# A gated mix of two attentions: one matmul per 128-row tile and PSUM bank for numerators and weight folds, where there were two

## The chip, the core and the metric

The kernel runs on one core of a Trainium2 chip. The core has five engines that run side by side, each through its own list of instructions in order: TensorE (PE) multiplies matrices, VectorE (DVE), ScalarE (ACT) and GpSimd (POOL) work on elements, SyncE (SP) issues DMAs. PE writes to PSUM, eight banks of 512 float32 columns; DVE and ACT read PSUM, POOL does not. The metric is the device time of one execution in microseconds (us); the lower the better.

## What is computed

Both halves take the same input x of 2048 tokens by 640 features, 32 heads of 20 features each.

```python
qkv = x @ wqkv                                   # half A: q, k, v by heads
pq, pk = q @ w_phi, k @ w_phi                    # per head, 20 x 20
phi = concat(softmax(p), softmax(-p))            # of pq and of pk
kv, z = phi_k^T v, sum over tokens of phi_k      # per head
a = ((phi_q @ kv) / (phi_q . z + 1e-6)) @ wo
...
# half B: four segments of 512 tokens; causal softmax attention within a segment,
# mixed per head (sigmoid(beta)) with a linear attention over the segments before; times its own wo
out = g * a + (1 - g) * b                        # g = sigmoid(sum(x * gate_w)) per token
```

All inputs and the output are bfloat16.

## The kernel before, in words

The kernel is one long program with no loops left at run time. The order of the instructions on each engine is the order in which the code emits them (a manual schedule over all engines); strings in the code spell out that order by hand.

**The 640 features as tiles and banks.** 640 features are five tiles of 128 rows (`KC = 5`, index `j`). Heads are 20 features wide, so a tile does not begin or end with a head: tile 0 holds heads 0 to 6, tile 1 heads 6 to 12, tile 2 heads 12 to 19, tile 3 heads 19 to 25, tile 4 heads 25 to 31 (`TH`, L62). Head 6 lies partly in tile 0 and partly in tile 1; heads 12, 19 and 25 are split in the same way. A product over all heads with a block-diagonal right side therefore takes, per tile, only the columns of that tile's heads, and the split heads need a sum over two tiles. The result of 640 columns lies in two PSUM banks, 16 heads (320 columns) each; tile 2 spans both.

`PIECES` (L63) lists these products: tile, bank, first head, end head. A product with `start` clears its bank's marks and writes; one without it follows in the same bank. In the list of before, a head that the tile before has begun is a product of its own (20 columns, added to what is there), and the heads that are new are another product. That makes ten products: 140, 20, 120, 20, 60 columns in bank 0 and 80, 20, 120, 20, 120 in bank 1. `FIRST` and `LAST` (L65) name the products that open and close a bank.

**Where the list is used.** `emit_foldM` (L186) multiplies a tile of a transposed weight matrix with the block-diagonal `w_phi` (`Wphi`), so that the projections deliver `pk` and `pq` at once; it is called ten times. Five calls are at the start for the keys (L317 on, steps M0, M2, M1, M4, M3; ACT casts each result into `WkA` at L194), five for the queries after the last key step (L348 on; ACT casts into `WqA`). `emit_num` (L477) multiplies a tile of the exponentials of the queries (`Eqs`) with the block-diagonal `kv` (`kvn`) for a chunk of 128 tokens and one sign: 16 chunks by 2 signs, 32 calls.

**What stands around the folds.** At the start PE transposes five tiles of the key weights (L182), with the folds in between, then multiplies x by the folded key weights and by the value weights, 16 steps of 20 products (L240). ACT takes the exponentials (L251) and copies the values (L253), DVE sums and takes reciprocals (L255, L258), POOL normalises (L259). After the sixteenth step come the five query folds, then the products `kv` (`emit_kv`, L394: short products of two column groups), in among them and after them the query products (`emit_pq`, L421) with their exponentials on ACT (L428). SP moves the normalised keys into `Z` (L267), DVE adds them (L275), and PE transposes the sum (L280).

**What stands around the numerators** (L647 to L706). In each of the 32 steps (chunk, sign) DVE scales a numerator (`emit_tt`, L531, into a tile `tt` with two buffers), PE does half of a projection for half B (five products of 320 columns, L561, which ACT casts at L621) and the numerator three steps ahead (three PSUM tiles of two banks: `nps0`, `nps1`, `nps2`). After both signs POOL adds the two halves (`oA`, L691) and SP transposes the sum. The denominators of the next batch of four chunks are made by PE behind two of the numerators (`emit_den`, L500), DVE takes their reciprocal (L507, L508) and that of their sum (L512, L694), and POOL makes the scale of the next batch from them (L522, L524), which `emit_tt` of the next batch needs. Then half B follows: scores on PE (L770), exponentials on ACT (L774), masks on POOL (L781), products with the values (L824), and the projections and outputs in between (L948, L1008).

Of the kernel before, what the change touches and what calls it, by code (L numbers as in the profile page):

```python
# [15 lines left out]
def kernel(  # L16
# [43 lines left out]


    TH = [(P * j // DH, (P * j + P - 1) // DH + 1) for j in range(KC)]  # L62
    PIECES = [(0, 0, 0, 7), (1, 0, 6, 7), (1, 0, 7, 13), (2, 0, 12, 13), (2, 0, 13, 16),  # L63
              (2, 1, 16, 20), (3, 1, 19, 20), (3, 1, 20, 26), (4, 1, 25, 26), (4, 1, 26, 32)]
    FIRST, LAST = {0, 5}, {4, 9}  # L65
    HW = 8

    gS = res.tile([P, NCH], F32, name="gS")
# [31 lines left out]
    for what in "c w1 w3 x0 x1 g v0 v1".split():  # L100
        n = int(what[1:]) if len(what) > 1 else 0
# [74 lines left out]
    def w2tile(name):  # L176
        return aps.tile([P, 2, 512], F32, name=name, tag="w2")
# [8 lines left out]
    def emit_foldM(WT, dst, ic, eng=nc.scalar.copy):  # L186
        ps = w2tile("fold_ps")
        for n, (j, bk, lo, hi) in enumerate(PIECES):
            h0 = TH[j][0]
            nc.tensor.matmul(ps[:, bk, (lo - 16 * bk) * DH:(hi - 16 * bk) * DH],  # L190
                             lhsT=WT[:, j, ic * P:(ic + 1) * P],
                             rhs=Wphi[:, j, lo - h0:hi - h0, :].rearrange("p h d -> p (h d)"),
                             start=(n in FIRST), stop=(n in LAST))
        eng(out=dst[:, ic, :].rearrange("p (b n) -> p b n", b=2), in_=ps[:, :, 0:320])  # L194

    def emit_xT(n):
# [120 lines left out]
    for step in "P T0a T2d M0a T1d M2a T4d T3d M1a X0 M4a X1 M3a k0 g k1 v0 v1 r0 r1".split():  # L317
        n = int(step[1:2] or 0)
        if step[0] == "T":
            emit_foldT(wnat_k, WkT, n, {"a": nc.scalar.copy, "d": nc.vector.tensor_copy}[step[2]])  # L320
        elif step[0] == "M":
            emit_foldM(WkT, WkA, n, {"a": nc.scalar.copy, "d": nc.vector.tensor_copy}[step[2]])
        elif step[0] == "X":
            emit_xT(n)
        elif step[0] == "P":
            for j in (0, 2):
                emit_Wphi(j, nc.vector)
        elif step[0] == "k":
            emit_a1_mm(n, pks, WkA, 320)
        elif step[0] == "v":  # L330
            emit_a1_mm(n, pvs, WvA, 321)
        elif step[0] == "r":
            emit_a1(n)
            emit_zmove(n)
        else:
            emit_gw()
# [11 lines left out]
    for n in range(KC):  # L348
        emit_foldM(WkT, WqA, n)
# [127 lines left out]
    def emit_num(ch, sgn):  # L477
        qb, qc = divmod(ch, HB // P)
        t = nps[(2 * ch + sgn) % 3].tile([P, 2, 512], F32, name="num")
        for n, (j, bk, lo, hi) in enumerate(PIECES):  # L480
            h0 = TH[j][0]
            nc.tensor.matmul(t[:, bk, (lo - 16 * bk) * DH:(hi - 16 * bk) * DH],  # L482
                             lhsT=Eqs[qb, j][:, sgn, qc * P:(qc + 1) * P],
                             rhs=kvn[:, sgn, j, lo - h0:hi - h0, :].rearrange("p h e -> p (h e)"),
                             start=(n in FIRST), stop=(n in LAST))
        return t

    def num_view(t):
# [161 lines left out]
    def emit_num_at(i):  # L650
        if i < len(order):
            ch, sgn = order[i]
            t = nums[ch, sgn] = emit_num(ch, sgn)
            if ch % 4 == 1 and ch < NCH - 4:
                for n in range(2):
                    emit_den(den_view(t)[:, n], ch + 3 + 2 * sgn + n)
# [55 lines left out]
    with ExitStack() as bctx:  # L712
# [487 lines left out]
        for ps, lo in quarters:  # L1200
            for k5 in range(KC):
                nc.tensor.matmul(ps, lhsT=oT4[:, 2, k5, :], rhs=WoB[:, k5, lo:lo + 160],
                                 start=(k5 == 0), stop=(k5 == KC - 1))
# [36 lines left out]
```

## Time and profile before

| what | value |
|---|---|
| three runs | 314.25, 313.38, 314.42 us |
| their median | 314.25 us |
| the profiled execution's own time | 314.52 us |
| its span | 312.8 us, 9844 instructions |
| granted TensorE clock | 1.0 |
| products at L482 (numerators) | 320, first and last start at 88.8 and 126.0 us |
| products at L190 (folds) | 100, first and last start at 5.2 and 55.1 us |

How to read the lines that follow. The page's first part gives for each engine the busy time, its share of the span and the number of instructions; PE is the matmuls, PEld the weight loads that belong to them. A group of instructions is shown with line, engine, operation, the tile that is written and the tiles that are read, shapes, count, busy time in us and mean duration of one in ns, then the idle time of the engine just before. The timeline gives start and duration in us, engine, line, operation, tiles, shapes and count, and in brackets the idle time before and what ended it. The chain of waits goes back from the last instruction to what released each one; its rows are start, duration, engine, tile, line and count. Where a distance between the starts of two single matmuls is given, it is from the start times in the same trace.

### The profile page before, as it was taken

The page shows a single profiled execution, that of the slowest core. Times are in us where ns is not written, and L with a number is a line of the kernel's source. Part 1 is how long each engine was busy: PE and PEld are TensorE (multiplying, and loading weights), DVE is VectorE, ACT ScalarE, POOL GpSimd, SP SyncE. Part 2 cuts the span into 40 slices and gives each one's busy share as a digit, 9 for nine tenths or more (in the row PEclk, how much of TensorE's full clock was granted, in tenths as well). Part 3 has the DMA queues.
Part 4 walks back from the last instruction along what each step waited for, and adds up shares of the span by engine and source line. Part 5 has one row for each costly group of instructions (what it writes and reads, how often), then busy time and mean ns, then how long its engine had stood idle before and what let it go on. Part 6 is the DMA issues. An engine that isn't in the chain of part 4 may idle for free.

```text
span 312.8 us, 9844 instructions
## 1 busy us (share of the span) xinstructions
PE 302.4 (97%) x4038; PEld 205.3 (66%) x4038; DVE 230.3 (74%) x532; ACT 251.9 (81%) x320; POOL 205.6 (66%) x310
## 2 busy tenths in 40 slices
PE   8999999999999999999999999999999999999995
PEld 7788877855578788465656666666666666544573
DVE  3477997998779997767758588788656746667773
ACT  4677888357956549899999899999998999899953
POOL 8588599103346989965666667688886767756560
PEclk9999999999999999999999999999999999999999
DMA  7989934439217998775331358343855556334142
GB/s 223 202 173 188 234 103 127 130 88 365 76 27 99 129 142 132 153 103 105 37 69 36 69 111 121 57 91 61 110 92 90 53 106 116 82 82 97 40 115 84
DMA packets 97414, 35.33 MB, mean 113 GB/s; under 512 B 85722, under 2 KB 97370, under 8 KB 97370
## 3 DMA queue, kind: packets, MB, share of 16 engines
q1 hardware_dynamic: 96794, 34.06, 56.3%
q10 hardware_dynamic: 576, 0.66, 0.7%
q8 instruction: 31, 0.51, 0.7%
q14 instruction: 13, 0.11, 0.1%
HBM read 6.10 MB, written 2.62 MB: 28 GB/s over the span
## 4 chain that ended last, share of the span: by engine, by line
PE 68%; ACT 21%; DVE 5%; POOL 3%; issue 2%; ACTq 0%; DVEq 0%; POOLq 0%
ACT PT L774 18%; PE proj L1008 10%; PE st_ps L770 9%; PE proj L948 8%; PE pq L421 7%; PE pk L240 7%; PE pv L240 7%; PE nda L824 5%; PE proj L561 3%; DVE tt L531 2%; PE num L482 2%; PE kv_ps L394 2%; DVE rr L507 2%; POOL oA L691 1%; PE warm L316 1%
## 5 line engine op out<-in xcount | busy, mean ns | idle before, releaser
L774 ACT ACTIVATE PT<-st_ps 128x1024 bf16<-128x1024 f32 x160 | 153.9, 1024 | 11.3 <-PE st_ps L770 8.9
L781 POOL TENSOR_SCALAR_AFFINE_SELECT PT<-PT 128x512 bf16<-128x512 bf16 (+1 forms) x130 | 83.8, 663 | 42.7 <-ACT PT L774 42.3
L259 POOL TENSOR_TENSOR EkSn<-Ek,krec 128x1280 bf16<-128x1280 bf16 x15 | 35.1, 2358 | 9.2 <-DVE krec L258 7.3
L824 PEld LDWEIGHTS <-PT 128*128 128x128 bf16 x1040 | 32.9, 96 | 7.8 <-issue 4.5
L1008 PEld LDWEIGHTS <-xTf 128*128 128x128 bf16 x300 | 26.5, 97 | 14.1 <-issue 5.5
L824 PE MATMUL nda<-vB,PT 128*128 128x21 bf16 x1000 | 34.2, 173 | 0.0
L1014 DVE CAST Z<-proj 128x320 bf16<-128x320 f32 x44 | 21.2, 489 | 16.4 <-PE proj L1008 15.3
L428 ACT ACTIVATE Eq<-pq 128x1024 bf16<-128x1024 f32 x20 | 19.4, 1021 | 12.6 <-PE pq L421 12.6
L255 DVE TENSOR_REDUCE ksum<-Ek 128x64 f32<-128x1280 bf16 x16 | 23.6, 1475 | 7.2 <-ACT Ek L251 7.2
L948 PE MATMUL proj<-WkA,oTA 128*128 128x320 bf16 x160 | 28.3, 300 | 0.0
L531 DVE TENSOR_TENSOR tt<-num,rr 128x640 f32<-128x640 f32 x32 | 25.0, 813 | 4.4 <-POOL rr L524 1.7
L770 PE MATMUL st_ps<-Z 32*128 32x512 bf16 (+3 forms) x256 | 25.2, 299 | 3.0 <-ACT PT L774 2.5
L691 POOL TENSOR_TENSOR oA<-tt 128x640 bf16<-128x640 f32 x16 | 24.6, 1546 | 5.2 <-DVE tt L531 5.0
L770 PE MATMUL st_ps<-Eq 32*128 32x384 bf16 (+3 forms) x256 | 25.6, 298 | 1.9 <-ACT PT L774 1.5
L251 ACT ACTIVATE Ek<-pk 128x640 bf16<-128x640 f32 x32 | 20.8, 703 | 8.1 <-PE pk L240 7.0
L240 PEld LDWEIGHTS <-xTf 128*128 128x128 bf16 x200 | 22.6, 113 | 4.7
L421 PE MATMUL pq<-xTf,WqA 128*128 128x512 bf16 x100 | 22.4, 379 | 0.3 <-issue 0.3
L948 PE MATMUL proj<-WvA,oT 128*128 128x320 bf16 x120 | 21.2, 300 | 0.0
L948 PEld LDWEIGHTS <-oTA 128*128 128x128 bf16 x160 | 13.5, 97 | 8.6 <-issue 4.6
L561 PEld LDWEIGHTS <-xTf 128*128 128x128 bf16 x180 | 15.8, 97 | 4.6
L770 PEld LDWEIGHTS <-Z 32*128 32x128 bf16 x256 | 7.5, 91 | 16.2 <-issue 15.0
L482 PEld LDWEIGHTS <-Eq 128*128 128x128 bf16 x320 | 15.9, 96 | 3.3 <-issue 0.7
(194 smaller groups left out, 584.8 us busy)
## 6 DMA issues: line engine op xcount, KB each, us to landing
Z<-EkSn SPq DMA_DIRECT2D x32, 160.0 KB, 2.8
out_dram<-orow SPq DMA_DIRECT2D x8, 160.0 KB, 1.8
out_dram<-oTA SPq DMA_DIRECT2D x6, 160.0 KB, 1.8
WvA<-in_A_wqkv_dram SPq DMA_DIRECT2D x2, 400.0 KB, 5.9
WvB<-in_B_wv_dram SPq DMA_DIRECT2D x1, 800.0 KB, 4.6
WkB<-in_B_wk_dram SPq DMA_DIRECT2D x1, 800.0 KB, 6.4
WqB<-in_B_wq_dram SPq DMA_DIRECT2D x1, 800.0 KB, 8.1
WkA<-in_A_wo_dram SPq DMA_DIRECT2D x1, 800.0 KB, 11.2
```

The costliest lines, as they stand in the source:

```text
L240: nc.tensor.matmul(ps[:, bk, 0:n], lhsT=key_tokens(c, sc), rhs=rhs, start=(c == 0), stop=(c == by_row[-1][0] if sc == 0 and W is WkA else ...
L259: (nc.vector if sc == NCH - 1 else nc.gpsimd).tensor_tensor(out=EkSn[:, sc].rearrange("p s (h f) -> p (s h) f", f=DH), in0=Ek.rearrange("p ...
L421: nc.tensor.matmul(pq[:, half, :], lhsT=WqA[:, c, j * P:(j + 1) * P], rhs=xq[:, 2 * qb + half, c], start=(c == 0), stop=(c == KC - 1))
L531: nc.vector.tensor_tensor(out=tt[:, sgn].rearrange("p (b h) d -> p b h d", b=2), in0=ps, in1=csb, op=ALU.mult)
L561: nc.tensor.matmul(ps, lhsT=xq[:, sc // 4, cc, sc % 4 * P:(sc % 4 + 1) * P], rhs=W[:, cc, half * 320:(half + 1) * 320], start=(cc == 0), s ...
L691: nc.gpsimd.tensor_tensor(out=oA.rearrange("p (h d) -> p h d", d=DH), in0=tt[:, 0], in1=tt[:, 1], op=ALU.add)
L770: nc.tensor.matmul(ps[:, i - i0, o:o + L - c * P], lhsT=kT[32 * i:32 * i + 32, c * P:(c + 1) * P], rhs=qT[32 * i:32 * i + 32, c * P:L], st ...
L774: nc.scalar.activation(out=PT[:, i0:i0 + 2], in_=ps, func=ACT.Exp, scale=SCALE_B)
L781: nc.gpsimd.affine_select(out=v, in_=v, pattern=[[0, n_i], [1, P]], compare_op=ALU.is_ge, fill=0.0, base=0, channel_multiplier=-1)
L824: nc.tensor.matmul(nd[:, j, i], lhsT=block(st, c)[:, i, (j - c) * P:(j - c + 1) * P], rhs=vB[:, c, 4 * st.g + i, :], start=(c == 0), stop= ...
L948: nc.tensor.matmul(ps, lhsT=oT[:, k % KC], rhs=W[:, k % KC, hs], start=(k == 0), stop=(k == n - 1))
L1008: nc.tensor.matmul(ps, lhsT=xq[:, sc // 4, k, sc % 4 * P:(sc % 4 + 1) * P], rhs=W[:, k, half * 320:(half + 1) * 320], start=(k == 0), stop ...
```

## The change

The list of products has six entries in place of ten: for each tile and bank, all heads of that tile that lie in the bank. Where the tile before has begun the first head, the product adds in that head's 20 columns and writes in the other columns, in one matmul. `FIRST` and `LAST` follow the new numbering. The matmuls of both functions carry `skip_group_check=True`. The columns in all stay 720 for each call; all other instructions stay, in their order.

```diff
     TH = [(P * j // DH, (P * j + P - 1) // DH + 1) for j in range(KC)]
-    PIECES = [(0, 0, 0, 7), (1, 0, 6, 7), (1, 0, 7, 13), (2, 0, 12, 13), (2, 0, 13, 16),
-              (2, 1, 16, 20), (3, 1, 19, 20), (3, 1, 20, 26), (4, 1, 25, 26), (4, 1, 26, 32)]
-    FIRST, LAST = {0, 5}, {4, 9}
+    PIECES = [(0, 0, 0, 7), (1, 0, 6, 13), (2, 0, 12, 16), (2, 1, 16, 20), (3, 1, 19, 26), (4, 1, 25, 32)]
+    FIRST, LAST = {0, 3}, {2, 5}
...
@@ emit_foldM
                              rhs=Wphi[:, j, lo - h0:hi - h0, :].rearrange("p h d -> p (h d)"),
-                             start=(n in FIRST), stop=(n in LAST))
+                             start=(n in FIRST), stop=(n in LAST),
+                             skip_group_check=True)
...
@@ emit_num
                              rhs=kvn[:, sgn, j, lo - h0:hi - h0, :].rearrange("p h e -> p (h e)"),
-                             start=(n in FIRST), stop=(n in LAST))
+                             start=(n in FIRST), stop=(n in LAST),
+                             skip_group_check=True)
```

## The prediction

> **What bounds the kernel now.** I read the page first, then the timeline of TensorE (PE), VectorE (DVE), GpSimd (POOL) and ScalarE (ACT) in the stretches where the edited lines run, and the chain of waits last.
>
> ```profile
> PE 302.4 (97%) x4038; PEld 205.3 (66%) x4038; DVE 230.3 (74%) x532; ACT 251.9 (81%) x320; POOL 205.6 (66%) x310
> q8 instruction: 31, 0.51, 0.7%
> ```
>
> PE is busy 97% of the span, but ends are modelled, so I go by starts. The second line is code: 31 packets, 0.51 MB. Over PE's 8076 instructions that is 63 bytes each, so queue 8 feeds PE, and one packet (16.4 KB) holds some 256 instructions, or 128 pairs of weight load and matmul. That matters below.
>
> The edited products, from the lines of the whole span, shapes kept apart:
>
> ```profile
> L482 PE MATMUL num<-kvn,Eq 128*128 128x120 bf16 x96 | 14.5, 213 | 0.0
> L482 PE MATMUL num<-kvn,Eq 128*128 128x20 bf16 x128 | 13.3, 173 | 0.0
> L190 PE MATMUL fold_ps<-Wphi,WkT 128*128 128x120 bf16 x30 | 4.7, 223 | 0.0
> L190 PE MATMUL fold_ps<-Wphi,WkT 128*128 128x20 bf16 x40 | 4.5, 183 | 0.0
> ```
>
> The 168 products of 20 columns are the ones to go: 128 at L482, 40 at L190. Their 173 ns is latency, not price; the price is the distance to the next start. In PE's timeline a numerator group of ten starts at 117.06 and the next work at 117.44. The starts inside it are 61, 28, 52, 26, 26, 35, 27, 52, 26 and 51 ns apart for 140, 20, 120, 20, 60, 80, 20, 120, 20 and 120 columns. So 20 columns cost 26 to 28 ns, 120 cost 52, 140 cost 61, and 60 cost as little as 20.
>
> Who sets the pace of the numerator stage (89 to 127 us) shows in DVE's timeline:
>
> ```profile
> 100.56 2.33 DVE L531 TENSOR_TENSOR tt<-num,rr 128x640 f32<-128x640 f32 x3 [0.55 <-POOL rr L524]
> ...
> 110.50 2.33 DVE L531 TENSOR_TENSOR tt<-num,rr 128x640 f32<-128x640 f32 x3 [0.57 <-POOL rr L524]
> ...
> 120.43 3.06 DVE L531 TENSOR_TENSOR tt<-num,rr 128x640 f32<-128x640 f32 x4 [0.56 <-POOL rr L524]
> 124.74 3.05 DVE L531 TENSOR_TENSOR tt<-num,rr 128x640 f32<-128x640 f32 x4 [1.25 <-POOL oA L691]
> ```
>
> A batch of four chunks takes 9.94 and 9.93 us, and in it DVE stands only in the waits for POOL that the brackets show. PE, in its timeline, waits for DVE:
>
> ```profile
> 116.00 0.54 PE L482 MATMUL num<-kvn,Eq 128*128 128x140 bf16 x10 [0.24 <-DVE uu L508]
> ```
>
> By the starts this wait is 0.40 us (the row before is modelled to run on), and 0.25 at 106.05. The loop DVE, POOL, DVE is the bound there; PE is close behind.
>
> **The change, part by part.** (1) *A product of 140 columns that writes and adds.* No row shows a mixed one. From below: 61 ns, the plain 140 row; it cannot be under the 52 ns of 120 columns. From above: 78 ns, the pair it replaces. Products that write and those that add have one price here (five products of 320 columns at L561 are 135, 135, 135, 136, 136 ns apart, the first of them writing), so I take 61. A group then takes 61+61+35+35+61+61 = 314 ns in place of 384: **0.07 us**, for 42 groups 2.9 us of PE. What counts is where it lies.
>
> (2) *The five folds of the key weights (5.2 to 9.4 us).* The chain of waits is PE with one ACT step here. Three groups run at the fast pace (7.63, 8.29, 8.95): 3 x 0.07. The first two (5.24, 6.38) run at half pace, 617 and 647 ns by starts: there 20+120 columns take 127 ns and 140 would take 117, so 4 x 10 ns each; and since the pace changes at a time and not at a product (about 7.2), half of that remains, 0.04 together. Gain 0.25. Cover: the keys' first product needs the last cast of WkA, which ACT ends at 10.23; its ninth matmul starts at 10.43. They move to about 10.12 and 10.18, so no new wait, with 0.06 to spare. After that PE is dense to 55 us, a step of 20 products each 2.73 us; the next input, a DMA transpose for the third step, lands at 14.1 for a need at 15.0. So 0.25 arrives.
>
> (3) *The five query folds (53.2 to 55.3).* 5 x 0.07 = 0.35 on PE, beside ACT. From 52.14 ACT is dense (two exponentials, a copy, five casts of WqA) until 57.12, and PE's fourth key-value tile waits for the last cast. In the chain:
>
> ```profile
> 53.45 0.69 ACT vA L253
> 54.15 1.27 ACT WqA L194 x3
> 55.79 1.34 ACT WqA L194 x2
> 57.18 4.00 PE kv_ps L394 x175
> ```
>
> Gain 0. It would be 0.35 were ACT faster.
>
> (4) *Code.* In the key-value burst that follows, matmuls start 18 ns apart, so a block of 128 lasts 2.3 us. PE stops in the query product right after it, waiting for nothing that the profile knows:
>
> ```profile
> 61.11 1.69 PE L421 MATMUL pq<-xTf,WqA 128*128 128x512 bf16 x7
> 63.05 0.81 PE L421 MATMUL pq<-xTf,WqA 128*128 128x512 bf16 x3 [0.26 <-issue]
> ```
>
> By starts 0.42 us is lost ahead of matmul 733 (counted from the first), and 0.12 ahead of matmul 605: 128 apart, one block. Queue 8's packets ran 55.97 to 57.42 and 60.27 to 61.52; PE went on at 58.8 and 63.05, 1.4 and 1.5 us after each ended. So from entering a block until the next is usable takes about 4.2 us (58.8 to 63.05). PE's sequencer leads by some 17 matmuls: at 50.86 it took the semaphore instruction of the query folds (matmul 426) while PE was at 409. Hence the block at 477 was entered when PE was at 460, at 54.75, and usable 4.0 later.
>
> The change takes 40 pairs out ahead of this burst, so the block limits fall on work that is now 517, 645 and 773. The first is entered with PE at 500, on today's clock 56.07; the next is usable at 60.1; PE is at 645 at 58.70 + 40 x 0.0184 = 59.43. **It stops for 0.65.** The one after is usable at 64.3, and PE gets to 773 at 60.1 + 1.47 + 0.13 + 2.16 + 0.77 = 64.6: no stop. So 0.65 for today's 0.54: a loss of 0.1. Ends: with no lead 0.95, with a refill of 3.7 us 0.35, so -0.2 to +0.4. Elsewhere blocks last 7 us or more.
>
> On the page "Runtime: NRT & Kernel Launch" (Instruction fetch mechanics) the Trainium skill gives PE's store as 2048 instructions, refilled in blocks of 256, and calls the crossing mostly hidden. The block agrees with 63 bytes x 256; the hiding does not agree with the gap of 0.42. By that page the folds' gain would stay whole.
>
> (5) *The 32 numerator groups: 2.2 us of PE.* Groups one and two end ahead of two projection halves, and the third group starts at 91.00 because ACT ends the last query exponential at 90.95: nothing. The third group and its denominators release the next tt at 92.15 (1.13 us idle): 0.07. From there to 124.7 the loop of DVE and POOL sets the pace, and 28 groups' 2.0 us turn into longer waits of PE. The last group starts at 125.62, held by the tt that waited for POOL's oA (the row at 124.74); after it come one projection and the next stage: 0.07.
>
> Sum on the path: -0.25 - 0.07 - 0.07 + 0.1 = **-0.3 us**. From 127 us on nothing is edited and all moves along. Of the profiled execution, 314.52 (span 312.8 and 1.7 around it), that leaves 314.2; the median shown is 314.25, 0.27 lower, and I carry the difference over: **314.0**. The three runs spread over 1.04 us, 0.33%, so about 0.3% (0.94 us) is what a measurement tells from no change.
>
> **Rivals.** *The code gaps vanish* (the limits fall kindly, or the refill is faster): -0.39 - 0.54 = -0.93, 313.3. For: the refill's first part varied (1.1 to 1.5 us). Against: a block in the burst lasts far less than any refill. Chance 0.15.
>
> *Crossings are hidden, and the 0.42 has another cause and stays*: -0.39, 313.9. For: no row names the cause. Against: the distance of exactly 128. This is what the skill's page above would give. Chance 0.12.
>
> *PE sets the numerator stage after all*: then up to 28 x 0.07 = 2.0 more, 312.0. For: in the chain PE holds 116 to 127 us almost alone. Against: DVE's rows above, and PE's waits for it. Chance 0.08.
>
> *Slower by a longer code stop*: should the moved limits meet two late refills, 1 us at 645 and 0.8 at 773, that is 1.8 - 0.54 - 0.39 = +0.9, 315.1. It makes the kernel slower from a sum of stops of 0.93. For: the refill would be asked for while the moves of Z load the DMA engines (56.4 to 60.6). Against: PE's ten long query products give 2.16 us before 773. Chance 0.15.
>
> *A mixed product costs as much as its pair*: only the limits of code move, +0.1 at most; without fewer instructions 314.25. For: no row shows one. Against: the equal prices in (1). Chance 0.05. That a product without the clearing flag adds where a cell was written and overwrites where it was not, I take from "PSUM — Partial Sum Buffer" (Terms) of the Trainium skill; no run here shows it yet.
>
> **Numbers.** My forecast (313.6 to 314.4) has 0.45. The range, 313.0 to 315.0, takes in the vanished gaps, the hidden crossings and the noise of the median, and leaves out the PE-bound case and the worse half of the longer stop. Faster by over 0.3%: the PE-bound case, half of the vanished gaps, some noise: 0.22. Slower: most of the longer stop and noise: 0.15. Within: 0.63.
>
> **What would show it.** Right: 192 products at L482, 60 at L190, PE x3870, no 20 columns; groups of 0.31 us; batches still 9.9 us apart at the same three rows of DVE with PE's waits for DVE longer, near 0.8 at the two places; the keys' products 0.25 earlier; the casts of WqA still dense; a stop of PE near the end of the key-value burst and none in the query product. Wrong: batches shorter than 9.8; a stop there of over 1 us or none; query folds that bring the key-value products forward.

## The result and the profile after

The changed kernel took 313.21 us (median of 22 runs, 312.93 to 314.31), the kernel before 313.96 in the same session (22 runs, 313.28 to 314.68): a ratio of 0.998, 95% interval 0.9973 to 0.9988. It is 0.75 us faster, 0.2%, which is inside the 0.3% that I had called no change. It lies in my range (313.0 to 315.0), under the 313.6 to 314.4 of my forecast, and next to the 313.3 of the rival in which the code gaps vanish. Two more sets of the unedited kernel are among the experiments; over all three the medians are 313.24 (46 runs) against 313.98 (74 runs), 0.74 us.

The profiled execution of the changed kernel took 313.52 with a span of 311.8 (before 314.52 and 312.8). The first part of its page, engines and the code queue:

```profile
PE 299.6 (96%) x3866; PEld 201.9 (65%) x3870; DVE 230.2 (74%) x532; ACT 251.2 (81%) x320; POOL 205.6 (66%) x310
q8 instruction: 30, 0.49, 0.7%
```

The weight loads show 168 products fewer; PE's 3866 are four short of them, records that the trace lacks. One packet of code less came in. The lines of the whole span, shapes apart, for the edited products (folds are now L189, numerators L482):

```profile
L482 PE MATMUL num<-kvn,Eq 128*128 128x140 bf16 x128 | 15.1, 224 | 1.5 <-DVE uu L509 1.1 <-DVE tt L532 0.2
L482 PE MATMUL num<-kvn,Eq 128*128 128x80 bf16 x64 | 7.5, 199 | 0.0
...
L189 PE MATMUL fold_ps<-Wphi,WkT 128*128 128x140 bf16 x40 | 4.4, 228 | 0.4 <-ACT WkT L183 0.2
L189 PE MATMUL fold_ps<-Wphi,WkT 128*128 128x80 bf16 x20 | 2.4, 200 | 0.0
```

No product of 20 columns is left. The first line has 1.5 us of waits, mostly for DVE, where before's row of this width had 0.3. In DVE's timeline the batches stand as they stood:

```profile
99.75 2.33 DVE L532 TENSOR_TENSOR tt<-num,rr 128x640 f32<-128x640 f32 x3 [0.55 <-POOL rr L525]
...
109.67 2.33 DVE L532 TENSOR_TENSOR tt<-num,rr 128x640 f32<-128x640 f32 x3 [0.55 <-POOL rr L525]
...
119.59 3.06 DVE L532 TENSOR_TENSOR tt<-num,rr 128x640 f32<-128x640 f32 x4 [0.55 <-POOL rr L525]
...
123.90 3.07 DVE L532 TENSOR_TENSOR tt<-num,rr 128x640 f32<-128x640 f32 x4 [1.25 <-POOL oA L692]
```

They are 9.92 and 9.92 us apart, and the waits for POOL are the same. PE's saved time became PE's wait, in its own timeline:

```profile
105.24 0.48 PE L482 MATMUL num<-kvn,Eq 128*128 128x140 bf16 x6 [0.55 <-DVE uu L509]
...
115.16 0.47 PE L482 MATMUL num<-kvn,Eq 128*128 128x140 bf16 x6 [0.55 <-DVE uu L509]
```

By the starts these waits are 0.72 us each, 0.25 and 0.40 before. A group's six starts are 61, 60, 35, 35, 63 and 61 ns apart, 0.31 us to the next work: **a product that writes and adds costs what a plain one of 140 columns costs.**

The stop for code is there, at another place. PE's timeline in the key-value burst (L394) and the query product behind it:

```profile
56.32 2.29 PE L394 MATMUL kv_ps<-vA,EkSn 128*128 128x140 bf16 x108
59.17 1.67 PE L394 MATMUL kv_ps<-vA,EkSn 128*64 128x80 bf16 x81 [0.55 <-issue]
60.77 2.33 PE L421 MATMUL pq<-xTf,WqA 128*128 128x512 bf16 x9
```

By starts 0.72 us is lost, ahead of matmul 605 as forecast (0.65), and none in the query product.

**Where the time went.** I cut the span at four events: K, the keys' first product; C, ScalarE's first cast of the query weights; G, the key-value product behind the ten query products; S, the first score product of the next stage. In us:

| profiled execution | K at | K to C | C to G | stops in C to G (at matmuls 605, 733) | G to S |
|---|---|---|---|---|---|
| before | 9.34 | 44.70 | 9.65 | 0.12, 0.42 | 63.08 |
| changed | 8.45 | 44.68 | 9.81 | 0.72, 0 | 62.93 |

So K to C is untouched, the numerators gave 0.15 (forecast 0.07 + 0.07), the code cost 0.16 (forecast 0.1), and the first nine microseconds gave 0.89 where I had 0.25. That was the first riddle. The second: if this execution still stops for 0.72 us, what do the others do that are faster (25 of the 46 took less than 313.42, down to 312.77)?

### The profile page after: what moved, and what is told of

Same layout as the page of the kernel before. It is cut to its first block, busy times and chain, and to the rows that moved or that the text cites. A ratio compares the mean times of both kernels' runs of the same rounds, so it can differ in the third digit from the quotient of the medians.

```text
span 311.8 us, 9504 instructions
## 1 busy us (share of the span) xinstructions
PE 299.6 (96%) x3866; PEld 201.9 (65%) x3870; DVE 230.2 (74%) x532; ACT 251.2 (81%) x320; POOL 205.6 (66%) x310
## 4 chain that ended last, share of the span: by engine, by line
PE 65%; ACT 21%; DVE 6%; POOL 4%; issue 2%; ACTq 0%; DVEq 0%; POOLq 0%
ACT PT L775 18%; PE proj L1009 10%; PE st_ps L771 10%; PE proj L949 8%; PE pk L240 7%; PE pq L421 7%; PE pv L240 7%; PE nda L825 5%; DVE tt L532 3%; POOL oA L692 2%; PE kv_ps L394 2%; DVE rr L508 2%; PE proj L562 1%; PE num L482 1%; PE warm L316 1%
## 5 line engine op out<-in xcount | busy, mean ns | idle before, releaser
L1009 PE MATMUL proj<-WkB,xTf 128*128 128x320 bf16 x110 | 18.0, 300 | 0.0
```

The lines of the kernel that those rows point to most:

```text
L1009: nc.tensor.matmul(ps, lhsT=xq[:, sc // 4, k, sc % 4 * P:(sc % 4 + 1) * P], rhs=W[:, k, half * 320:(half + 1) * 320], start=(k == 0), stop ...
```

## The experiments

Theory A: the products give what they cost (0.2 in the key folds, 0.14 at the numerators' two ends, nothing in the query folds), and what is beyond that is code: 40 pairs fewer ahead of the burst move the block limits off places that cost 0.54 us. Theory B: fewer products give the whole gain, wherever the limits lie. This is the form that both had from e9 on; the expectations of the runs ahead of it say what A and B meant there. The ratios are those on record, from all executions of a set; they are not quotients of the medians.

**One part at a time.** The list of ten and the list of six are both kept, and each use picks one:

```diff
+        pieces, FIRST, LAST = SIX if dst is WkA else TEN    # e1_keys: key folds alone
+        pieces, FIRST, LAST = TEN if dst is WkA else SIX    # e2_queries: query folds alone
...
+        pieces, FIRST, LAST = SIX                           # e3_nums: numerators alone, folds TEN
```

> Only the five key folds use the six products; query folds and numerators keep ten. Theory A (the prediction's: 0.07 us a group, 0.25 us for the keys on the path; the surplus of the whole change, measured 0.75 us against 0.3, is chance in when TensorE goes from half to full pace in the profiled execution): -0.25 for the folds, and 20 pairs of code fewer ahead of the key-value burst, so a stop of about 0.7 us ahead of matmul 605 and none at 733 (+0.15): -0.1 us, ratio 0.9997. Theory B (the key folds themselves make the full pace come sooner, so the surplus belongs to them): -0.5 to -0.6 us, ratio about 0.9983.

Measured 313.27 against 314.01, ratio 0.9977 (0.9967 to 0.9987), and no stop at all in the profile, where I had expected one of 0.7. The edit takes 20 pairs out ahead of the burst, and it alone gives what the whole change gives. That is nearer to the 0.9983 of B as it stood there (the key folds make the full pace come sooner); the clock times further down speak against that B.

> Only the five query folds use the six products. By the prediction their 0.35 us lie beside ScalarE's dense casts: 0, and the code's limits move by 20 pairs as in the run with the keys alone: a stop of about 0.7 us ahead of matmul 605, none at 733: +0.15 us, ratio 1.0005. Rival (TensorE sets the pace there): -0.35 + 0.15 = -0.2 us, and the key-value products start 0.35 us earlier against the last cast of WqA.

Measured 313.59 against 314.01, ratio 1.0002 (0.9984 to 1.002): by itself unresolved, since three of its 12 executions, at 315.2 to 315.7, show a mean granted clock of 0.993, as the profiled execution of e3 does, which had a stretch at half of TensorE's clock (told below); the other nine have a median of 313.58. The profile has no stop, against what I expected, and took 312.96. ScalarE's casts stayed dense, so the query folds themselves gave nothing.

> Only the 32 numerator groups use the six products; all folds keep ten, so nothing before 88 us changes, the stops of 0.12 and 0.42 us at matmuls 605 and 733 included. By the prediction 0.07 us at the third group and 0.07 us at the last: -0.14 us, ratio 0.9995, with batches still 9.9 us apart. Rival (TensorE sets the numerator stage): -2.2 us, ratio 0.993. If the surplus of the whole change sat here: about -0.6 us.

Measured 314.13 against 314.01, ratio 1.0004 (0.9987 to 1.0021). Nothing moves ahead of the burst here, and both stops are there: 0.37 and 0.41 us. G to S is 62.94, as in the changed kernel. The 0.14 is in the profile and too small for the times.

**Idle products that shift the limits.** Short products whose result lies in PSUM columns that nothing reads stand behind the query folds, where PE waits for ScalarE anyway. In e4_fill14, 14 of them behind the third and the fifth fold of the changed kernel:

```diff
+        for _ in range(14 if dst is WqA and ic in (2, 4) else 0):
+            nc.tensor.matmul(ps[:, 0, 340:356], lhsT=WT[:, 0, ic * P:(ic + 1) * P],
+                             rhs=Wphi[:, 0, 0:1, 0:16].rearrange("p h d -> p (h d)"),
+                             start=True, stop=True, skip_group_check=True)
         eng(out=dst[:, ic, :].rearrange("p (b n) -> p b n", b=2), in_=ps[:, :, 0:320])
```

> The changed kernel with 14 idle products of 16 columns (into unused columns of the fold's own PSUM tile) after the third and after the fifth query fold, where TensorE waits for ScalarE. 28 pairs of code come back ahead of the key-value burst, so the block limits at matmuls 605 and 733 fall on work 28 pairs earlier than in the changed kernel. If the stop is code (theory A): the stop at 605 shrinks from 0.72 to about 0.25 us, none at 733, and the time is 0.4 to 0.5 us below the changed kernel, about 312.8 us. If the stop has another cause at a fixed piece of work: it stays 0.7 us at the same product, and the time is that of the changed kernel or up to 0.1 us more.

Measured 313.23 against 314.01, ratio 0.9979 (0.9965 to 0.9994), no stop. Already 12 pairs off the limits of before there is none; my model of the refill had 0.25. The time is that of the changed kernel, and not the 312.8 expected, which took the stop of 0.72 for the rule.

The changed kernel unedited, in a second set:

> The changed kernel once more, unedited, to see whether its stop of 0.72 us ahead of matmul 605 comes again. Theory A (the stop comes from where the block limit falls): 0.6 to 0.8 us there in this execution too; time about 313.2 us, ratio about 0.998. Rival (the stop is chance of one execution, typical executions have none, and this is where the surplus of the gain comes from): below 0.2 us or absent.

Measured 313.23 against 314.09, ratio 0.9975 (0.9961 to 0.9988). **The stop of 0.72 did not come again**: PE's timeline of this execution runs through the place in one row. That is the rival of this expectation.

```profile
56.40 3.87 PE L394 MATMUL kv_ps<-vA,EkSn 128*128 128x140 bf16 x190
60.20 2.33 PE L421 MATMUL pq<-xTf,WqA 128*128 128x512 bf16 x9
```

So the same program stops in one execution and not in another. Now code alone, on the kernel before: 12 idle products behind its third and its fifth query fold (`range(12 if ...)` in the diff above), every product of the change undone.

> The kernel before with 12 idle products of 16 columns after the third and after the fifth query fold: nothing of the change, only 24 pairs of code more ahead of the key-value burst, hidden in TensorE's waits for ScalarE there. Block limits at matmuls 605 and 733 fall on work that is 581 and 709 in the kernel before. If the stops are code: no stop at 605, and at 733, inside the burst, 1.0 to 1.5 us in place of 0.12 + 0.42: +0.5 to +0.9 us, ratio 1.002 to 1.003. If the stops have another cause: as before, ratio 1.000.

Measured 315.46 against 314.09, ratio 1.0047 (1.0029 to 1.0066). In PE's timeline the limit now falls at the end of the burst:

```profile
56.32 3.81 PE L398 MATMUL kv_ps<-vA,EkSn 128*128 128x140 bf16 x179
61.19 0.49 PE L398 MATMUL kv_ps<-vA,EkSn 128*64 128x80 bf16 x17 [1.05 <-issue]
```

By starts 1.22 us at matmul 733, as expected. Idle work that lies almost wholly behind ScalarE made the kernel slower by the code it pushes. (C to G is 0.81 longer than before: 0.68 by the stops and 0.14 by the idle products themselves. The time rose by 1.37, more than the 0.5 to 0.9 expected; in the profiled execution another 0.60 lies behind S, where among the outputs SP's three issues took 2.21 us for 1.31. Why is open.)

**The key folds at full pace.** To have all five groups run at the fast pace, the identity that the transposes wait for comes later, behind eight memsets, and a longer warm-up fills the time; with ten and with six products:

```diff
-    for n in range(20):
-        nc.tensor.matmul(warm[n % 2][:, 0, 0:160], ...
+    for n in range(24):
+        nc.tensor.matmul(warm[n % 2][:, 0, 0:512], ...
...
+    for _ in range(8):
+        nc.gpsimd.memset(idle, 0.0)      # and only then ident_b
```

> The kernel before with the identity matrix made late (about 9 us) and 24 warm products of 512 columns in place of 20 of 160, so that every execution enters the key folds at TensorE's full pace. To be compared with its twin. Expected: some 6 us above the kernel before (about 320 us), a smaller spread than 1.4 us; the five key folds at 0.38 us each.

> The same with the six products. Theory A (the gain of the key folds is that of the products, 0.2 to 0.35 us, and the rest of the measured 0.75 us is the time at which the pace changes): first key product 0.2 to 0.35 us earlier than in the twin, and the time lower by 0.2 to 0.4 us by the folds and numerators, plus or minus what the stops of code differ. Theory B (the surplus does not hang on the pace): 0.7 us lower with equal stops.

Measured 322.33 and 320.27, ratios 1.0266 (1.0239 to 1.0293) and 1.0199 (1.0179 to 1.0219). They do not tell the folds' worth: in the profile of e7 the clock's record falls to half from 11.13 to 14.54, in the middle of the folds, after 3.42 us in which PE, held up by the late identity, was busy for only 1.11; in e8 it does not fall. The design failed. Of use is one thing: with four products more ahead of everything, the stops lie again at matmul 605 (0.24 in e7; 0.23 in e8, which has 36 pairs fewer than before ahead of it) and, in e7, in the query product (1.20 by starts, ahead of matmul 733 again).

**The limits put back.** The test that parts the theories: keep every product that the change saves, and put idle ones in their place, so that the limits fall where they fell before. Eight behind each of the five query folds of the changed kernel make up the 40; four behind each make up the 20 of the key folds alone; and four in the changed kernel leave the limits 20 off. The unedited kernel ran beside them a third time.

```diff
-        for _ in range(14 if dst is WqA and ic in (2, 4) else 0):
+        for _ in range(8 if dst is WqA else 0):      # e9; 4 in e10 and e11
```

> The changed kernel with eight idle products of 16 columns behind each of the five query folds (40 products, about 0.2 us each time, beside ScalarE's casts; their results lie in PSUM columns that nothing reads). With them the limits of TensorE's code blocks lie on the same products of the key-value burst as in the kernel before (matmuls 605 and 733), while every product that the change saved stays saved. Theory A (the change is worth 0.34 us by its products, the rest by the code limits that move away from the burst's bad places): stops of 0.3 to 0.7 us at 605 and 733 together come back in the profile, and the time is 0.3 to 0.4 us under that of the kernel before: ratio 0.9989. Theory B (all of the gain comes from fewer products, wherever the limits lie): no stop, ratio 0.9975 as in the changed kernel.

> Six products in the key folds alone, and four idle products of 16 columns behind each query fold (20 in all), so that the code limits lie as in the kernel before. Theory A (key folds are worth 0.2 us at an equal pace of TensorE, the other 0.54 that this edit gave without the idle products was the code): 0.2 to 0.25 us under the kernel before, ratio 0.9993, and stops of 0.3 to 0.7 us at matmuls 605 and 733 together. Theory B (the key folds themselves are worth 0.74, by stages that then fall together better): ratio 0.9977, as without the idle products.

> The changed kernel with four idle products of 16 columns behind each query fold: the limits lie 20 pairs off those of the kernel before, where the kernels with one kind of fold alone had no stop. Theory A: no stop, 0.85 to 0.9 us under the kernel before, ratio 0.9972, and as fast as the changed kernel or 0.1 faster (if that still stops in some executions). Theory B: as the changed kernel, 0.9975.

> The changed kernel unedited, a third time. Two profiles so far: one with a stop of 0.72 us at matmul 605, one without. Theory A: 0.75 to 0.85 us under the kernel before, ratio 0.9975; a stop of 0 to 0.7 us at 605, none at 733. Theory B says nothing of the stop, and the same time.

| kernel | limits | median (before: 313.96) | ratio (95%) | stops at 605, 733 |
|---|---|---|---|---|
| e9, change + 40 idle | as before | 313.77 | 0.9998 (0.9988 to 1.0008) | 0.17, 0.42 |
| e10, key folds + 20 idle | as before | 313.74 | 0.9998 (0.9985 to 1.0011) | 0.13, 0.41 |
| e11, change + 20 idle | 20 off | 313.35 | 0.9988 (0.9976 to 1.0001) | none |
| e12, change | 40 off | 313.56 | 0.9997 (0.9984 to 1.0009) | none |

The query product in e9 and then in e12, from PE's timeline:

```profile
61.02 1.69 PE L425 MATMUL pq<-xTf,WqA 128*128 128x512 bf16 x7
62.96 0.81 PE L425 MATMUL pq<-xTf,WqA 128*128 128x512 bf16 x3 [0.26 <-issue]
```

```profile
56.49 3.88 PE L394 MATMUL kv_ps<-vA,EkSn 128*128 128x140 bf16 x190
60.29 2.33 PE L421 MATMUL pq<-xTf,WqA 128*128 128x512 bf16 x10
```

The rows of before are back, 1.69, 0.81 and the gap of 0.26, and gone again where the limits are moved. Theory B had 0.9975 for e9 and 0.9977 for e10, and both intervals exclude these. But so does that of e12, the unedited kernel beside them: 0.9997, for 0.9975 expected and 0.998 and 0.9975 in the two sets ahead of it. The ratios of this set therefore do not part the theories. e11, too, is 0.6 us under before for 0.85 to 0.9 expected. Part is known: two of 12 executions of each had a lower granted clock, 0.993 (314.1 to 314.9). The rest is open; the medians of this set separate A's two cases by only 0.2 to 0.4 us, and the profiles carry the verdict.

Over all sets the medians do sort by the limits. Against the kernel before in the same set they are +0.12, -0.19 and -0.22 us for the three kernels with the limits as before (e3, e9, e10), -0.40 to -0.86 for the seven medians with 12 to 40 pairs fewer, and +1.37 for e6. The nearest pair, e1 and e10, has the same six-product key folds and differs by the 20 idle products: -0.74 and -0.22. Idle products as such do not cost that: e4 with 28 and e11 with 20 have -0.78 and -0.60.

Over all profiles but the two of e7 and e8, which start later:

| profiled | K at | K to C | C to G less stops | stops at 605, 733 | G to S |
|---|---|---|---|---|---|
| *limits as before:* before | 9.34 | 44.70 | 9.11 | 0.12, 0.42 | 63.08 |
| e3 | 8.56 | 44.68 | 9.12 | 0.37, 0.41 | 62.94 |
| e9 | 8.99 | 44.70 | 9.32 | 0.17, 0.42 | 62.93 |
| e10 | 8.36 | 45.09 | 9.17 | 0.13, 0.41 | 63.06 |
| *24 pairs more:* e6 | 8.61 | 44.70 | 9.25 | 0, 1.22 | 63.06 |
| *12 to 40 pairs fewer:* changed | 8.45 | 44.68 | 9.09 | 0.72, 0 | 62.93 |
| e1 | 8.94 | 44.70 | 9.08 | none | 63.06 |
| e2 | 8.54 | 44.68 | 9.07 | none | 63.06 |
| e4 | 8.86 | 44.68 | 9.08 | none | 62.93 |
| e5 | 8.55 | 44.70 | 9.11 | none | 62.93 |
| e11 | 8.35 | 44.86 | 9.11 | none | 62.95 |
| e12 | 8.64 | 44.70 | 9.11 | none | 62.92 |

Read by columns: G to S is 63.06 to 63.08 with ten products in the numerators and 62.92 to 62.95 with six, 0.14 us, in every one of the twelve. The stop at 733 is 0.41 or 0.42 in all four kernels with the old limits and absent in the seven with fewer pairs. (e9's 9.32 is 0.2 that its 40 idle products cost.) Beside the stops K is what scatters (K to C only in e10 and e11, told below), and that answers the first riddle. The trace's record of TensorE's full clock begins at 7.09 us in before and at 5.47 in the changed kernel, and the products' spacing changes with it. Sorted by that time:

| products in the key folds | full clock from: K at |
|---|---|
| ten | 3.84: 8.54; 5.26: 8.56; 5.36: 8.61; 7.09: 9.34 |
| six | 4.34: 8.35; 5.17: 8.36; 5.47: 8.45; 5.70: 8.55; 5.93: 8.64; 6.48: 8.86; 6.65: 8.94; 6.76: 8.99 |

At one clock time the six-product folds are 0.2 us earlier (5.17 and 5.26; 5.47 and 5.36 with 0.04 for the clock); the other 0.7 of the 0.89 was when the clock rose in those two executions. The full clock comes at 4.34 to 6.76 with six products and at 3.84 to 7.09 with ten, so the six do not bring it sooner.

## Why the prediction came out as it did, point by point

**(1) The mixed product: right.** 60 to 63 ns, and a group of 0.31 us.

**(2) The key folds: mechanism right, 0.2 for 0.25.** The chain of waits of the changed kernel shows them on the path:

```profile
5.24 0.59 PE fold_ps L189 x6
5.82 0.28 PE wtp L181 x5
6.10 0.32 PE fold_ps L189 x6
6.42 0.62 PE wtp L181 x10
7.04 0.32 PE fold_ps L189 x6
```

The saving is partly eaten by two waits of 0.07 us, which I had not counted; each ends 0.05 us after a cast of `WkA` on ScalarE (the casts end at 6.55 and 8.09). "So no new wait" also fails at the far end in the two executions with the earliest K, e10 and e11. They wait for an input in their third step, here in e10's timeline:

```profile
14.42 1.55 PE L249 MATMUL pk<-WkA,xTf 128*128 128x320 bf16 x10 [0.23 <-DMA xTf<-in_A_x_dram]
```

Their K to C is 45.09 and 44.86. That transfer bounds what a faster start can bring; I had put it 0.9 us ahead of its need.

**(3) The query folds: right.** In the chain of the changed kernel ScalarE still carries the place:

```profile
53.23 1.20 ACT WqA L194 x3
...
54.87 1.34 ACT WqA L194 x2
...
56.26 2.35 PE kv_ps L394 x97
58.61 0.55 issue
59.17 1.67 PE kv_ps L394 x81
```

**(4) Code: the term that was mis-sized.** I said "0.65 for today's 0.54: a loss of 0.1". The places were right: limits 128 matmuls apart, the gap in the query product gone, the new one at 605. In the profiled execution even the size was (0.72), by luck: of three profiles of the unchanged program two have no stop, and "none" stood among my signs of being wrong. The four kernels with 12 to 20 pairs fewer have none either; e8, with 36 fewer, has 0.23. The more common value is thus 0, a gain of 0.54, which is the rival that I gave 0.15.

What failed is "usable 4.0 later". Counted from C, PE reached matmul 605 in the changed kernel at 5.3 us (0.72 later than before; I had 0.73). My 60.1 was 6.06 on that scale. Queue 8's packet ended at 3.37 to 3.61 in the four kernels with the old limits, and PE went on 1.36 to 1.39 after its end in each. In e5 and e12 it ended at 4.03 and 3.91; with the same 1.37 the block is usable at about 5.40 and 5.28, just when PE needs it. The kernels with 12 to 20 pairs fewer come there at 4.8 to 4.9, and by the same sum their block was usable at 4.7 to 5.0, so they pass with little to spare. In the execution with the stop the packet ended at 4.42 and PE went on 1.62 later, at 6.04. From matmul 460, where I put the entry, to 605 it is 4.06 us in that execution and, without a stop, 3.36 in e5 and e12, the same program: the refill varies by at least 0.7 us, and I had taken about 4, from one execution, for its size. (The kernel before has 4.20 there, since its product 460 started at 54.57 and not at my 54.75.) Whether the entry or the transfer varies, and why, is open.

The rule that I weighed there, from "Runtime: NRT & Kernel Launch" of the Trainium skill (Instruction fetch mechanics), that crossings are mostly hidden, holds for two of three profiles of the changed kernel and not for the kernel before or e6, which stopped 0.54 and 1.22 us. The rival made from it (the 0.42 stays, from another cause) is out: the gap goes and comes with the limits alone.

**(5) The numerators: right.** 0.14 us at the two ends, nothing from 28 groups; the rivals of a PE-bound stage and of a dearer product are out.

**The sum.** -0.2 - 0.14 - 0.54 = -0.88 us without a stop; with the stop of the first profile -0.16. The sets measured -0.75, -0.86 and -0.40. On my forecast of 314.0 the code term alone makes it 313.4; the kernel before at 313.96 in the session, and not at the 314.25 of the three runs, takes another 0.3 from it. What remains unsettled is small: from S to the end the kernels with fewer pairs took 185.88 to 185.94 us, before 186.03, e10 186.07, e9 186.35 and e6 186.63, perhaps code again in the last burst; no run tells.

## What to carry to other kernels

Where short matmuls stand 18 ns apart, a block of 128 pairs is gone in 2.3 us and its refill is not, so removing or adding matmuls ahead of such a burst moved the stops here; put the old limits back with idle products before crediting a gain to the work that was saved. Merging products buys PE time only where PE ends last: 168 products gave 0.34 us, and the code limits that they moved gave 0.54 where no new stop came. And a term read from one gap in one execution needs its spread from a second profile before it goes into a sum.

## What the runs showed of the hardware beside that

The time at which TensorE's pace doubles is not set by the kernel: 3.84 to 7.09 us in twelve executions with the same warm-up, worth up to 0.8 us at K. And in some executions the clock falls to half for one stretch in mid-kernel: in e3's profile from 203.23 to 206.64, 3.41 us, after which everything is 1.5 us later. PE had been busy for 3.20 of the 3.41 us ahead of it; in e7, whose fall came after 1.11 busy us of 3.42, the idle time is plain. Executions with the same mean granted clock as e3's, 0.993 to 0.995, came with the kernel before as well (4 of the 35 beside e1 to e4, at 314.6 to 315.6). From the start of the full clock to the fall it is 58.0 times 3.41 us in e3 and 2.0 times in e7. The Trainium skill, "TensorE: Matmul & The Clock Gate" (What's actually happening), gives a window of 3413 ns that runs freely and does not begin anew with a kernel; these rows agree with it. Its variation of 500 ns either way does not agree with the 3.25 us between the earliest and the latest time here. Why e3 lost a window after one that was so nearly full, no run here shows.
